# One query tile of a weights load goes as sixteen rows of 16 KB to partitions 0 to 15

## The chip, the cores and the metric

The kernel runs on one core of a Trainium2 chip. The metric is the device time of one execution in microseconds. A core has engines that run side by side: TensorE (PE, with its weight loads shown as PEld), VectorE (DVE), ScalarE (ACT), GpSimd (POOL) and SyncE (SP), which issues transfers. Sixteen DMA engines move the data between HBM and the on-chip memory of 128 partitions.

## What is computed

Two layers, each an attention over a cached sequence and a token-mixing MLP, with a residual around each, for a batch of 2 with one new token (`D = 512`):

```python
q = (x @ wq).reshape(B, Sq, Hq, Dh).transpose(0, 2, 1, 3)      # B 2, Sq 1, Hq 32, Dh 128
k, v = repeat(k_cache, 4, axis=1), repeat(v_cache, 4, axis=1)  # caches: 2 x 8 x 32768 x 128
p = softmax(einsum("bhqd,bhkd->bhqk", q, k) * Dh ** -0.5)
o = einsum("bhqk,bhkd->bhqd", p, v).transpose(0, 2, 1, 3).reshape(B, Sq, Hq * Dh) @ wo
...
x = x + A(layernorm(x), k_cache, v_cache, wq, wo)
x = x + mixer(layernorm(x), w1, b1, w2, b2)
x = x + A(layernorm(x), k_cache, v_cache, wq, wo)
x = x + mixer(layernorm(x), w1, b1, w2, b2)
```

All is float32. The two caches are 268 MB each, and both layers read them.

## The kernel before

The work is cut into 32 units, one for each layer, batch row and key head. A unit has eight chunks of keys and eight of values, 2 MB each. The four query heads of a key head are the rows of one product, so a unit needs the four queries of its head and, at its end, its head's part of the output matrix.

One large tile `mem` in the on-chip memory holds everything that is loaded. It is divided into cells of 4096 columns (16 KB in a partition): cells 0 to 8 are the ring for keys and values, cells 9 to 12 (`WCELL0`, `WCELLS`) hold weights, and 2560 columns more (`REST`) lie behind them. Most loads are four chunks at once: 128 rows of 64 KB, 8 MB. They go in one queue, SyncE's, in the order keys of a unit (4 chunks), values of the unit before (4 chunks), and so on. A load that overwrites a buffer waits on SyncE until PE has worked through what lay there; while it waits, what stands behind it on SyncE waits too.

`load_weights(k, cell)` loads the weights of two heads (`TWO_HEADS[k]`) as one transfer of 128 rows of 32 KB, 4 MB: for each head four query tiles (128 rows of `wq` by 512 columns, `DT` of them) and four output tiles (`R`). `wq_at(h)` and `wo_at(h)` find them again through `home`. The pairs 0 to 2 are loaded once in each layer, the pair 3 stays: seven loads.

The queries of a unit are made by `make_q` in four steps. Steps 0 and 1 are `q_products` with two tiles each: a matmul with the normalised input (`xnT`, 128 rows by one or two batch rows) against a query tile, 512 columns wide, summed over the four tiles into one bank. Steps 2 and 3 copy the row and turn it into columns (`L362`, `L366`, `L374`). Both batch rows of a head are made at once.

The order is written down by a small planner at build time: time is counted in chunks, `kbeg[n]` is the time of unit n's first chunk of keys, `at(time, f, ...)` notes a call, and the last loop goes through the chunks, issues each load, works off each chunk (`k_chunk` with the scores, `L426`; `v_chunk`, `L581`) and calls what is noted for that time. So steps 0 and 1 of the query for unit n stand at `kbeg[n] - 6` and `kbeg[n] - 5`, behind the second and third chunk of four chunks of keys, and a weights load stands at `kbeg[n] - 10`. On each engine the instructions run in that order.

`spot()` hands out rows of 512 columns for passing results, eight in turn in cell 8. `misc()` hands out parts of one bank.

Of the kernel before, what the change touches and what calls it, by code (L numbers as in the profile page):

```python
# [13 lines left out]
P = 128  # L14
CK = 4096
# [5 lines left out]
RING = 3  # L21
# [7 lines left out]
REST = 5  # L29
IN_PSUM = (4, 5, 3)  # L30
KEPT_Q = 4
RESIDENT = (5, 7)
TWO_HEADS = ((0, 1), (2, 3), (4, 6), RESIDENT)
FOLLOWS = {2: (2.2, -0.9, -0.8, -0.7, 3.5, -0.6, -0.5, -0.4), 5: (3.05, 0.1, 0.2, 0.3, 5.1, 3.1, 3.2, 3.3)}
PIECES = (32, 16, 8, 4, 4)
THIN = 16
# [8 lines left out]
def gqa_mixer_kernel(ctx: ExitStack, tc: tile.TileContext, x, kt, v, wqo, cols, out):  # L45
# [17 lines left out]
    nc = tc.nc  # L63
    B, D = out.shape
# [4 lines left out]
    R = wqo.shape[2] // (4 * D)  # L69
    DT = D // P  # L70
# [19 lines left out]
    sm, w0 = {}, 0  # L90
# [7 lines left out]
    W = wqo.shape[2] // 4  # L98
    assert CK == 2 * W
    WCELL0, WCELLS = RING * RING, 4  # L100
    heads = list(range(HKV))
    passing = [h for h in heads if h not in RESIDENT]
    home = {}
    mem = const.tile([P, (WCELL0 + WCELLS) * CK + REST * QT * DH], F32, name="mem")

    def cells(k, m=1):
        return mem[:, k * CK : (k + m) * CK]

    def wq_at(h):
        return cells(home[h])[:, :W].rearrange("p (t c) -> p t c", t=DT)  # L110

    def wo_at(h):
        return cells(home[h])[:, W:].rearrange("p (t c) -> p t c", t=R)

    def load_weights(k, cell):
        for j in range(2):
            home[TWO_HEADS[k][j]] = cell + j
        nc.sync.dma_start(cells(cell, 2), wqo[k])


    busy = [0] * 2 * (WCELL0 + WCELLS + 1)
    now = [0]
# [72 lines left out]
    ident = sm["ident"]  # L195
# [84 lines left out]
    N1 = len(units) - 1  # L280
# [5 lines left out]
    N3 = len(units) - 1  # L286
# [7 lines left out]
    xnT = sm["xn"].rearrange("p (d b) -> p d b", b=B)  # L294
# [5 lines left out]
    spots = [0]  # L300

    def spot():

        spots[0] += 1
        return cells(RING * RING - 1)[:, spots[0] % (CK // D) * D :][:, :D]

    def to_columns(key):

# [12 lines left out]
    def unit_of(n):  # L321

        return units[n]

    q_ps, q_row, q_kept = {}, {}, {}
    kept_q = [0]

    def partner(n):

        layer, b, h = unit_of(n)  # L330
        return units.index((layer, B - 1, h)) if b == 0 and (layer == 0 or h in passing) else None

    def q_products(n, *ds):

        layer, b, h = unit_of(n)
        m = 1 if partner(n) is None else B
        for d in ds:
            if d == 0:
                q_ps[n] = bcast if N1 < n <= N3 + 2 else kept[0]
            nc.tensor.matmul(  # L340
                q_ps[n][:m, :],
                xnT[:, d, b : b + m],
                wq_at(h)[:, d, :],
                start=(d == 0),
                stop=(d == DT - 1),
            )

    def make_q(n, step, place=None):

# [8 lines left out]
        if step < 2:  # L358
            q_products(n, 2 * step, 2 * step + 1)
# [329 lines left out]
    ln = sm["ln"]  # L689
# [238 lines left out]
    kbeg, k_done, vbeg, v_done, vend_of, v_from, v_to, brings, starts, t = {}, {}, {}, {}, {}, {}, {}, [], [], 0  # L928
# [13 lines left out]
    def at(time, f, *a, rank=1):  # L942
        done.setdefault(time, []).append((rank, f, a))

    HC = NCH // HALVES
    opens = {two[0]: k for k, two in enumerate(TWO_HEADS)}
    mixed = {}
    for n in range(NU):
        layer, b, h = unit_of(n)
# [19 lines left out]
                assert max(v_done[n - 2, c] for c in range(HC)) <= q2  # L969
        if n and h in opens and (units[n] == (0, 0, h) or h in passing and units[n] == (1, 0, h)):  # L970
            at(kbeg[n] - (7 if n == N3 + 2 else 10), load_weights, opens[h], WCELL0 + opens[h] % 2 * 2)
        if n in (N1 + 1, N2 + 1):
            at(kend - 0.5, turn_scores, n, 0, rank=2)
            at(kend, q_products, n + 1, 0)
            at(kend, max_1, n)
            at(kend, q_products, n + 1, 1)
            at(kend, max_2, n)
            at(kend, exponentials_at_once, n, 0)
            at(kend, q_products, n + 1, 2, 3)
            t1 = kend + 2  # L980
            assert mixed[units[n - 1][:2]] == kend == kbeg[n + 1] - 2
            at(t1, turn_scores, n, 1, rank=2)
            at(t1, exponentials_at_once, n, 1, rank=2)
            at(t1 + 1, sums, n)
            assert t1 + 1 < v_done[n, HC] - 1
        else:
            t1 = max(kend + 2, ahead + (2 if urgent else 4))
            e = kend if N1 < n <= N3 else kend + 2
            at(max(kend, e - 1), max_1, n)
            at(e, max_2, n)  # L990
            t0 = max(k_done[n, HC - 1], *(v_done[n - 1, c] for c in range(HC) if n), 0)
            if n in (N2, N3):
                t0 = max(t0, kbeg[n + 1] - 3)
            at(t0, turn_scores, n, 0)
            at(e, exponentials, n, 0)
            if n == NU - 1:
                t1 = ahead
                assert t1 >= kend + 2 and vbeg[n] == ahead
            at(t1, turn_scores, n, 1)
            at(t1, exponentials, n, 1)  # L1000
# [74 lines left out]
    t = 0  # L1075
# [11 lines left out]
    assert not done, sorted(done)  # L1087


def _layout(A_x, A_k_cache, A_v_cache, A_wq, A_wo, B_w1, B_b1, B_w2, B_b2):  # L1090

    import numpy as np

    B, HKV, SK, DH = A_k_cache.shape
    D = A_x.shape[-1]
    n = SK // CK


    keys = np.arange(SK).reshape(n, CK)
    for c0, m in GROUPS:  # L1100
        keys[c0 : c0 + m] = keys[c0 : c0 + m].reshape(P, m, CK // P).transpose(1, 0, 2).reshape(m, CK)
    k = keys.reshape(n // PACK, PACK // 2, 2, NG, 32, JT // QT, QT // SUB, SUB)
# [11 lines left out]
    return {  # L1114
        "x": np.ascontiguousarray(A_x.reshape(B * (D // P), P).T),
        "kt": kt,
        "v": A_v_cache.reshape(B * HKV, SK * DH),
        "wqo": np.stack([np.concatenate([wqo[h] for h in two], axis=1) for two in TWO_HEADS]),
        "cols": np.concatenate(cols, axis=1),
    }  # L1120

# [24 lines left out]
```

## Time and profile before

| | |
|---|---|
| runs | 2490.39, 2491.54, 2491.6 us; median 2491.54 |
| the profiled execution | 2490.09 us, its span 2488.0 us |
| mean granted TensorE clock | 0.772 |
| busy PE, PEld, DVE, ACT | 1371.4, 376.2, 244.9, 187.7 us |
| moved | 1062.51 MB, 427 GB/s on the mean |
| `L426` (scores) | x4096, 631.7 us busy |
| `L581` (values) | x4088, 596.8 us busy |
| `L340` (query products) | x104 into `kept`, x40 into `bcast` |

The page gives the busy time of each engine, then the span in forty slices, the DMA queues, the chain of work that ended last, and groups of instructions by line. A float32 matmul stands as two records, so 2048 matmuls of scores are 4096 rows. The timeline merges equal instructions that follow each other; a number in brackets is the idle time of the engine ahead of them. The idle time of an engine that isn't the bottleneck costs nothing.

### The profile page before, as it was taken

Reading aid. Unit: us, or ns where it says so; the run is one execution under the profiler, and the core shown is the slowest. Engines: PE = TensorE matmul, PEld = TensorE weight load, DVE = VectorE, ACT = ScalarE, POOL = GpSimd, SP = SyncE. Lnnn points to the kernel's source line nnn. Section 1 sums busy time; section 2 is a strip of 40 time slices with the busy share of each in tenths; the row PEclk is TensorE's granted clock in tenths of the full one; section 3 lists DMA queues with packets and bytes.
Section 4 is the critical chain, followed back from the end, with each engine's and each line's share of the span. In section 5 each row is a group of like instructions: output and inputs, shape, how many; then the busy total and the mean of one; then the engine's idle time right before and its main releaser. Section 6 shows DMA issues by size and latency. Waiting matters only on the chain.

```text
span 2488.0 us, 20543 instructions
## 1 busy us (share of the span) xinstructions
PE 1371.4 (55%) x9302; PEld 376.2 (15%) x9302; DVE 244.9 (10%) x643; ACT 187.7 (8%) x554; POOL 4.9 (0%) x17
## 2 busy tenths in 40 slices
PE   4544445544545454657677665455455465455546
PEld 1111111111111111111121121111111111111112
DVE  1000000000000000003113110000000000010002
ACT  0000000000000000002012000000000000011002
POOL 0000000000000000000000000000000000000000
PEclk8777767876777777778888887777678677777878
DMA  9999999999999999999999999999999999999996
GB/s 421 437 432 428 433 436 430 434 435 427 436 436 432 426 436 431 427 431 407 433 427 417 428 432 432 438 430 431 432 428 438 428 429 435 431 434 431 432 431 291
DMA packets 30336, 1062.51 MB, mean 427 GB/s; under 512 B 3621, under 2 KB 3625, under 8 KB 4266
## 3 DMA queue, kind: packets, MB, share of 16 engines
q1 hardware_dynamic: 29960, 1061.17, 99.1%
q8 instruction: 73, 1.20, 0.2%
q14 instruction: 13, 0.11, 0.0%
q10 hardware_dynamic: 290, 0.04, 0.0%
HBM read 1061.19 MB, written 0.00 MB: 427 GB/s over the span
## 4 chain that ended last, share of the span: by engine, by line
DMA 73%; PE 25%; DVE 1%; issue 0%; another core or an unknown queue 0%; ACT 0%; SPq 0%; POOL 0%; ACTq 0%
DMA mem<-in_v_dram 64%; PE acc L581 20%; DMA mem<-in_kt_dram 9%; PE scores L426 3%; PE small L612 0%; PE small L455 0%; PE small L449 0%; PE bcast L340 0%; ACT S L466 0%; PE small L642 0%; PE kept L246 0%; PE kept L792 0%; PE bcast L672 0%; DVE S L551 0%
## 5 line engine op out<-in xcount | busy, mean ns | idle before, releaser
L426 PE MATMUL scores<-mem,small_sb 128*32 128x512 f32 x4096 | 631.7, 736 | 605.4 <-DMA mem<-in_kt_dram 605.2
L581 PE MATMUL acc<-mem,S 128*16 128x512 f32 x4088 | 596.8, 723 | 457.1 <-DMA mem<-in_v_dram 447.7
L426 PEld LDWEIGHTS scores<-mem,small_sb 128*32 128x32 f32 x4096 | 150.0, 129 | 988.7 <-issue 903.7
L466 ACT ACTIVATE S<-S,small_sb 128x128 f32<-128x128 f32 x240 | 123.4, 517 | 2107.9 <-DVE small_sb L457 1556.9
L581 PEld LDWEIGHTS acc<-mem,S 128*16 128x16 f32 x4088 | 132.6, 109 | 810.8 <-issue 664.4
L441 DVE TENSOR_REDUCE small_sb<-scores 128x1 f32<-128x512 f32 x64 | 44.2, 691 | 819.5 <-PE scores L426 819.5
L461 DVE STREAM_TRANSPOSE S<-scores 128x512 f32<-128x512 f32 x64 | 45.5, 710 | 116.0 <-PE acc L581 116.0
L340 PE MATMUL kept<-mem,small_sb 128*2 128x512 f32 x104 | 51.1, 617 | 1.7 <-DVE small_sb L274 1.7
L466 ACT ACTIVATION_READ_ACCUMULATOR S<-S,small_sb 128x1 f32 x240 | 44.7, 186 | 0.0
L246 PE MATMUL kept<-mem,small_sb 128*1 128x512 f32 (+1 forms) x236 | 42.4, 598 | 2.6 <-ACT mem L835 2.4
L451 DVE TENSOR_REDUCE small_sb<-small 1x4 f32<-1x128 f32 x32 | 8.9, 279 | 277.7 <-PE small L449 277.7
L614 DVE RECIPROCAL small_sb<-small 128x4 f32<-128x4 f32 x32 | 5.9, 185 | 304.6 <-PE small L612 304.6
L623 DVE TENSOR_TENSOR small_sb<-small,small_sb 128x4 f32<-128x4 f32 x31 | 5.1, 164 | 295.8 <-PE small L621 295.8
L551 DVE SCALAR_TENSOR_TENSOR S<-acc,small_sb,S 128x128 f32<-128x128 f32 x93 | 32.6, 351 | 3.3
L835 ACT ACTIVATE S<-bcast,small_sb 128x512 f32<-128x512 f32 x28 | 21.5, 777 | 87.2 <-DVE small_sb L704 85.1
L366 PE MATMUL small<-small_sb,mem 2*128 2x2 f32 x112 | 15.5, 256 | 17.9 <-DVE mem L362 17.9
L549 DVE TENSOR_SCALAR S<-acc,small_sb 128x128 f32<-128x128 f32 x31 | 10.8, 350 | 147.3 <-PE acc L581 147.3
L621 PEld LDWEIGHTS small<-small_sb,S 128*128 128x128 f32 x62 | 12.7, 258 | 48.8 <-issue 41.2
L340 PE MATMUL bcast<-mem,small_sb 128*1 128x512 f32 (+1 forms) x40 | 19.4, 600 | 0.0
L366 PEld LDWEIGHTS small<-small_sb,mem 2*128 2x128 f32 x112 | 14.3, 196 | 30.5 <-DVE mem L362 27.3
L852 DVE SCALAR_TENSOR_TENSOR acc<-S,small_sb,acc 128x512 f32<-128x512 f32 x24 | 18.1, 755 | 2.5
L449 PE MATMUL small<-small_sb 128*1 128x128 f32 x64 | 16.6, 353 | 3.1 <-DVE small_sb L447 3.1
(147 smaller groups left out, 285.3 us busy)
## 6 DMA issues: line engine op xcount, KB each, us to landing
mem<-in_kt_dram SPq DMA_DIRECT2D x14, 4096.0 KB, 22.5
mem<-in_v_dram SPq DMA_DIRECT2D x11, 4096.0 KB, 29.2
mem<-in_wqo_dram SPq DMA_DIRECT2D x7, 4096.0 KB, 37.6
mem<-in_v_dram SPq DMA_DIRECT2D x13, 2048.0 KB, 21.3
mem<-in_kt_dram SPq DMA_DIRECT2D x12, 2048.0 KB, 19.3
mem<-in_kt_dram SPq DMA_DIRECT2D x24, 1024.0 KB, 8.8
mem<-in_v_dram SPq DMA_DIRECT2D x21, 1024.0 KB, 8.8
mem<-in_kt_dram SPq DMA_DIRECT2D x2, 6144.0 KB, 24.2
```

Of the source, the lines that this page charges most:

```text
L246: nc.tensor.matmul((rows if to is None else to)[32 * g : 32 * g + b + 1, :], weights if b else weights[:, 1:], row, start=to is not None, ...
L340: nc.tensor.matmul(q_ps[n][:m, :], xnT[:, d, b : b + m], wq_at(h)[:, d, :], start=(d == 0), stop=(d == DT - 1),)
L366: nc.tensor.matmul(pt[:, r * m : (r + 1) * m], q_row[n][:m, r * DH : (r + 1) * DH], ident[:m, :m], start=True, stop=True,)
L426: nc.tensor.matmul(sc_ps[n, half][32 * g : 32 * g + 32, :], q, kc[k * NG + g], start=(i == 0 and k == 0), stop=(i == PACK - 1 and k == SUB ...
L441: nc.vector.tensor_reduce(mx[n][:, half : half + 1], sc_ps[n, half], axis=AX.X, op=ALU.max)
L449: nc.tensor.matmul(pm[:1, :P], mxa, ident, start=True, stop=True)
L461: nc.vector.transpose(S[half], sc_ps[n, half])
L466: nc.scalar.activation(s[:, :, h], s[:, :, h], AF.Exp, bias=neg[n][:, h : h + 1], scale=SCALE, accum_out=lsum[n][:, half, h : h + 1],)
L551: nc.vector.scalar_tensor_tensor(t, acc[:, k * DH : (k + 1) * DH], mask[:, k : k + 1], t, op0=ALU.mult, op1=ALU.add)
L581: nc.tensor.matmul(acc[32 * g : 32 * g + R * QT, :], S[half][:, col : col + R * QT], vc[q], start=(c == v_from[n] and q < NG), stop=(c == ...
L835: nc.scalar.activation(hid[key, f], px[key], AF.Gelu_apprx_tanh, bias=shift[key][:, f : f + 1], scale=slope[key][:, f : f + 1],)
L852: nc.vector.scalar_tensor_tensor(h if f == FT - 1 else acc, h, w, acc, op0=ALU.mult, op1=ALU.add)
```

## The change

For the pairs 1 and 2 (`PART`: heads 2 and 3, heads 4 and 6), in both layers, one of the sixteen tiles leaves the weights load: the fourth query tile of the pair's first head. The load is then 128 rows of 30 KB. The tile, 128 rows of 512 columns, is laid out in HBM as sixteen rows of 4096 columns: row u holds the tile's rows u, u + 16, u + 32, ... one behind the other. `lower_tile` brings them to partitions 0 to 15 of cell 8, in four loads of four rows (partitions step, step + 4, step + 8, step + 12), one at a time at `kbeg[n] - 28`, `- 24`, `- 20` and `- 16`.

So that the product can be made, the input's last 128 rows go to partitions 0 to 15 as well: `lower_input` makes eight products with sixteen columns of the identity each and copies the result to `low`, a part of the mixer's small columns. The product for this tile is then a sum of eight, each over 16 rows. `spot()` hands out cell 8 only from unit N1 (13) to unit N3 + 4 (22), where cell 8 isn't used for the tile, and five rows of the columns behind the weights otherwise.

```diff
+PART = (1, 2)
+Q = 16
...
+    lowered = {}
+    low = sm["ln"][:Q, 16 : 16 + P // Q * B]
...
     def load_weights(k, cell):
+        tiles = 2 * (DT + R) - (k in PART)
         for j in range(2):
-            home[TWO_HEADS[k][j]] = cell + j
-        nc.sync.dma_start(cells(cell, 2), wqo[k])
+            home[TWO_HEADS[k][j]] = cell * CK + j * (DT + R - (k in PART)) * D
+        of = wqo[k].rearrange("p c -> (p c)")[: P * tiles * D].rearrange("(p c) -> p c", p=P)
+        nc.sync.dma_start(mem[:, cell * CK :][:, : tiles * D], of)
+
+    def lower_tile(k, step):
+        to = mem[:Q, (WCELL0 - 1) * CK :][:, : P // Q * D]
+        lowered[TWO_HEADS[k][0]] = to
+        of = wqo[k].rearrange("p c -> (p c)")[-P * D :].rearrange("(u c) -> u c", u=Q)
+        nc.sync.dma_start(to[step::4], of[step::4])
+
+    def lower_input():
+        p = misc()
+        for a in range(P // Q):
+            nc.tensor.matmul(
+                p[:Q, a * B : (a + 1) * B], ident[:, a * Q : (a + 1) * Q], sm["xn"][:, -B:], start=True, stop=True
+            )
+        nc.vector.tensor_copy(low, p[:Q, : P // Q * B])
...
     def spot():
         spots[0] += 1
-        return cells(RING * RING - 1)[:, spots[0] % (CK // D) * D :][:, :D]
+        inside = kbeg[N1] <= now[0] < kbeg[N3 + 4]
+        w, m = ((WCELL0 - 1) * CK, CK // D) if inside else ((WCELL0 + WCELLS) * CK, REST)
+        return mem[:, w + spots[0] % m * D :][:, :D]
...
-            nc.tensor.matmul(
-                q_ps[n][:m, :],
-                xnT[:, d, b : b + m],
-                wq_at(h)[:, d, :],
-                start=(d == 0),
-                stop=(d == DT - 1),
-            )
+            pairs = [(xnT[:, d, b : b + m], wq_at(h, d))] if h not in lowered or d < DT - 1 else [
+                (low[:, a * B + b : a * B + b + m], lowered[h][:, a * D : (a + 1) * D]) for a in range(P // Q)
+            ]
+            for i, (x, t) in enumerate(pairs):
+                nc.tensor.matmul(
+                    q_ps[n][:m, :], x, t, start=(d == 0), stop=(d == DT - 1 and i == len(pairs) - 1)
+                )
...
             at(kbeg[n] - (7 if n == N3 + 2 else 10), load_weights, opens[h], WCELL0 + opens[h] % 2 * 2)
+            if opens[h] in PART:
+                at(kbeg[n] - 28, lower_input)
+                for step in range(4):
+                    at(kbeg[n] - 28 + 4 * step, lower_tile, opens[h], step)
```

On PE, ahead of the unit that opens with head 2 in the first layer, the query products stood between the scores of the second, third and fourth chunk like this (`kept` is the bank of the queries, `acc` that of the values):

```order
L426 MATMUL scores<-mem,small_sb 32x512 x16
L340 MATMUL kept_85<-mem,small_sb 2x512 x2
L426 MATMUL scores<-mem,small_sb 32x512 x8
L340 MATMUL kept_85<-mem,small_sb 2x512 x2
L426 MATMUL scores<-mem,small_sb 32x512 x8
L366 MATMUL small<-small_sb,mem 128x2 x4
L581 MATMUL acc<-mem,S_91 16x512 x8
```

With the change (its lines are numbered otherwise: `L453` are the scores, `L371` the query products, `L393` the turn into columns, `L608` the values) the same place on PE reads:

```order
L453 MATMUL scores<-mem,small_sb 32x512 x16
L371 MATMUL kept_85<-mem,small_sb 2x512 x2
L453 MATMUL scores<-mem,small_sb 32x512 x8
L371 MATMUL kept_85<-mem,small_sb 2x512 x9
L453 MATMUL scores<-mem,small_sb 32x512 x8
L393 MATMUL small<-small_sb,mem 128x2 x4
L608 MATMUL acc<-mem,S_91 16x512 x8
```

The second group has nine matmuls where it had two; it stands ahead of the scores of the last chunk. The same is so at the other three places.

On SyncE's queue, the loads ahead of the same unit were these (`in_kt_dram` keys, `in_v_dram` values, `in_wqo_dram` weights):

```order
L139 DMA mem<-in_kt_dram 128x16384
L139 DMA mem<-in_v_dram 128x16384
L139 DMA mem<-in_kt_dram 128x16384
L139 DMA mem<-in_v_dram 128x16384
L139 DMA mem<-in_kt_dram 128x16384
L139 DMA mem<-in_v_dram 128x16384
L118 DMA mem<-in_wqo_dram 128x8192
L139 DMA mem<-in_kt_dram 128x16384
```

With the change (`L164` keys and values, `L126` weights, `L134` the four loads of rows):

```order
L164 DMA mem<-in_kt_dram 128x16384
L134 DMA mem<-in_wqo_dram 4x4096
L164 DMA mem<-in_v_dram 128x16384
L134 DMA mem<-in_wqo_dram 4x4096
L164 DMA mem<-in_kt_dram 128x16384
L134 DMA mem<-in_wqo_dram 4x4096
L164 DMA mem<-in_v_dram 128x16384
L134 DMA mem<-in_wqo_dram 4x4096
L164 DMA mem<-in_kt_dram 128x16384
L164 DMA mem<-in_v_dram 128x16384
L126 DMA mem<-in_wqo_dram 128x7680
L164 DMA mem<-in_kt_dram 128x16384
```

Each small load stands behind a load of 8 MB and ahead of the next one; the weights load has 7680 columns for 8192. Besides these, PE gets eight small products and DVE one copy four times; the order of all else is as it was.

More of the change, by code (lines that the diff above doesn't have):

```diff
@@ L107, in cells, with wq_at @@
         return mem[:, k * CK : (k + m) * CK]
-    def wq_at(h):
-        return cells(home[h])[:, :W].rearrange("p (t c) -> p t c", t=DT)
+    lowered = {}
+    low = sm["ln"][:Q, 16 : 16 + P // Q * B]
+    def wq_at(h, d):
+        return mem[:, home[h] + d * D :][:, :D]
     def wo_at(h):
-        return cells(home[h])[:, W:].rearrange("p (t c) -> p t c", t=R)
+        w = home[h] + (DT - (h in lowered)) * D
+        return mem[:, w : w + W].rearrange("p (t c) -> p t c", t=R)
     def load_weights(k, cell):
+        tiles = 2 * (DT + R) - (k in PART)
         for j in range(2):
-            home[TWO_HEADS[k][j]] = cell + j
-        nc.sync.dma_start(cells(cell, 2), wqo[k])
+            home[TWO_HEADS[k][j]] = cell * CK + j * (DT + R - (k in PART)) * D
[13 more added lines that the diff above has]
+        nc.vector.tensor_copy(low, p[:Q, : P // Q * B])
     busy = [0] * 2 * (WCELL0 + WCELLS + 1)
@@ L1087, in gqa_mixer_kernel, with _two_heads @@
     assert not done, sorted(done)
+def _two_heads(two, parted, d):
+    import numpy as np
+    if not parted:
+        return np.concatenate(two, axis=1)
+    c = np.arange((d // P - 1) * d, d // P * d)
+    main = np.concatenate([np.delete(two[0], c, axis=1), two[1]], axis=1)
+    last = two[0][:, c].reshape(P // Q, Q, d).transpose(1, 0, 2)
+    return np.concatenate([main.ravel(), last.ravel()]).reshape(P, -1)
 def _layout(A_x, A_k_cache, A_v_cache, A_wq, A_wo, B_w1, B_b1, B_w2, B_b2):
@@ L1117, in _layout @@
         "v": A_v_cache.reshape(B * HKV, SK * DH),
-        "wqo": np.stack([np.concatenate([wqo[h] for h in two], axis=1) for two in TWO_HEADS]),
+        "wqo": np.stack([_two_heads([wqo[h] for h in two], k in PART, D) for k, two in enumerate(TWO_HEADS)]),
         "cols": np.concatenate(cols, axis=1),
```

## The prediction

> **What bounds the kernel now.** I read the page first: its DMA rows, then the chain of waits.
>
> ```profile
> span 2488.0 us, 20543 instructions
> DMA  9999999999999999999999999999999999999996
> q1 hardware_dynamic: 29960, 1061.17, 99.1%
> q8 instruction: 73, 1.20, 0.2%
> DMA 73%; PE 25%; DVE 1%; issue 0%; another core or an unknown queue 0%; ACT 0%; SPq 0%; POOL 0%; ACTq 0%
> mem<-in_wqo_dram SPq DMA_DIRECT2D x7, 4096.0 KB, 37.6
> ```
>
> The transfers of SyncE's queue fill 99.1% of all sixteen engines' time, in every slice but the last. The kernel is a stream; it gets shorter only if the engine that finishes last has less to move, and longer if that stream runs dry. The 25% of PE in the chain is the work that frees a buffer before the next load can be issued; it costs nothing while an earlier load is still moving.
>
> The last microseconds of the stream, in a table of stretches (length, busy time of PE, PEld, DVE, ACT and POOL with instructions in brackets, PE clock, DMA share, GB/s), show that the sixteen engines don't finish together.
>
> ```profile
> 2466.00:2467.00 1.00, 0.57 (x8) 0.25 (x12) 0.00 (x0) 0.00 (x0) 0.00 (x0) 1.00 0.92 367
> 2467.00:2468.00 1.00, 1.00 (x16) 0.12 (x4) 0.00 (x0) 0.00 (x0) 0.00 (x0) 1.00 0.59 240
> 2469.00:2470.00 1.00, 0.95 (x8) 0.03 (x6) 0.00 (x0) 0.00 (x0) 0.00 (x0) 1.00 0.48 188
> 2470.00:2471.00 1.00, 0.80 (x24) 0.43 (x24) 0.91 (x3) 0.00 (x0) 0.00 (x0) 1.00 0.33 123
> ```
>
> The share falls from 0.92 to 0.48, half the engines, about 3 to 4 us before the rest stop. So some engines have spare time, which rows given to them could use.
>
> The change touches four places, the query products of the pairs that begin with heads 2 and 4, in both layers. I read the first in the timeline (start, length, engine, line, operation, and in brackets the idle time before it and what ended it), then the chain there.
>
> ```profile
> 218.77 0.43 SPq L118 DMA_DIRECT2D mem<-in_wqo_dram  x1
> 276.02 6.31 PE L426 MATMUL scores<-mem,small_sb 128*32 128x512 f32 x32 [19.72 <-DMA mem<-in_kt_dram]
> 285.57 1.45 PE L340 MATMUL kept<-mem,small_sb 128*2 128x512 f32 x3
> 286.86 0.59 PE L340 MATMUL kept<-mem,small_sb 128*2 128x512 f32 x1
> 289.25 0.33 SPq L139 DMA_DIRECT2D mem<-in_kt_dram  x1
> 295.37 3.44 PE L581 MATMUL acc<-mem,S 128*16 128x512 f32 x16 [3.73 <-DMA mem<-in_v_dram]
> ...
> 295.23 0.14 issue
> ```
>
> The 4 MB of weights have just held up the keys' load, and PE idles 19.72 us for it. At 276.02 the keys have landed and only one transfer, the values' 8 MB, is still queued; it lands at 295.23 (the last row is the chain's: landing, then 0.14 us to the matmul). Its 19.35 us are all the cover that PE has to work through four chunks of keys and the query products. SyncE can issue the next load only when that is done, at 289.25. This leaves 5.98 us. The same stands at the other three places:
>
> ```profile
> 610.11 0.33 SPq L139 DMA_DIRECT2D mem<-in_kt_dram  x1
> 616.23 3.44 PE L581 MATMUL acc<-mem,S 128*16 128x512 f32 x16 [3.73 <-DMA mem<-in_v_dram]
> ...
> 1794.39 0.33 SPq L139 DMA_DIRECT2D mem<-in_kt_dram  x1
> 1800.38 3.58 PE L581 MATMUL acc<-mem,S 128*16 128x512 f32 x16 [3.60 <-DMA mem<-in_v_dram]
> ...
> 1958.79 0.33 SPq L139 DMA_DIRECT2D mem<-in_kt_dram  x1
> 1965.32 3.62 PE L581 MATMUL acc<-mem,S 128*16 128x512 f32 x16 [3.92 <-DMA mem<-in_v_dram]
> ```
>
> With 0.14 us off the matmul's start, the landings are 616.09, 1800.24 and 1965.18, and the time left is 5.98, 5.85 and 6.39 us.
>
> **The change part by part.** *The weights load* loses 128 of its rows of 2 KB, 256 KB in all. The values' 8192 KB move in 19.35 us (276.02 to 295.37), so 256 KB are 0.60 us. Four times that is a gain of 2.4 us on every engine, and the most that the change can bring, since no other byte goes away.
>
> *The sixteen rows of 16 KB.* The 8 MB load has 128 rows of 64 KB, eight to an engine, 2.42 us each; a 16 KB row takes 0.60 us. What matters is which engines move them. The one transfer of the trace with four rows is the output's, and this is its window:
>
> ```profile
> DMA packets 8, 0.00 MB, mean 1 GB/s; under 512 B 4, under 2 KB 8, under 8 KB 8
> ```
>
> Eight packets: four of 512 B and four smaller ones, which I read as one count of the semaphore for each engine. Four rows went to four engines, then, and not to sixteen. If the four loads use the same four engines, these get 4 x 0.60 = 2.4 us more and 0.6 less, +1.8 us at each place, while the other twelve get -0.6. [...] If the four were among those with spare time, the landing at each place moves by -0.6; if they were among the last, by +1.8. But a lead is lost when the stream runs dry, which the next paragraph expects at each place, and then they have little to give at the next. I take the middle, +0.6 a place, +2.4 in all, with -2.4 and +7.2 as the ends.
>
> *The query products.* In step 1 of the first head of each pair, two matmuls of 512 columns become nine: seven more. A float32 matmul stands in the trace as two records, and the four records of the two old products start 0.43 us apart (285.57, three of them, and 286.86). Seven more are 14 x 0.43 = 6.0 us. They contract over 16 rows where those did over 128, and no row shows that shape; the columns that stream through are as many, so I take the same price. Above it lies 14 x 0.59 = 8.3 us, were they not to overlap; below it, little, were they to run side by side. The clock at the place is full:
>
> ```profile
> 276.00:282.00 6.00, 5.98 (x32) 1.65 (x33) 0.00 (x0) 0.00 (x0) 0.00 (x0) 0.55 1.00 429
> 286.00:288.00 2.00, 2.00 (x18) 0.61 (x17) 0.00 (x0) 0.00 (x0) 0.00 (x0) 1.00 0.83 360
> ```
>
> PE is busy without a gap in both, so nothing hides them; the idle 19.72 us lie ahead of the keys and can't be used, since the order is fixed. The scores of the last chunk are queued behind them on PE, SyncE's load waits for these scores, and the sixteen engines wait for SyncE. The issue moves from 289.25 to 295.3, when the values have just landed: the 5.98 us are gone.
>
> An issue isn't a transfer. What a start from an empty queue costs, the beginning of the run shows:
>
> ```profile
> 0.74 0.39 SPq L118 DMA_DIRECT2D mem<-in_wqo_dram  x1
> 1.00:1.70 0.70, 0.00 (x0) 0.00 (x0) 0.32 (x2) 0.04 (x1) 0.53 (x5) 1.00 0.00 0
> 1.70:2.00 0.30, 0.00 (x0) 0.00 (x0) 0.27 (x3) 0.30 (x1) 0.00 (x0) 1.00 4.47 1201
> 1.19 31.32 DMA mem<-in_kt_dram
> ```
>
> Issued at 0.74, the first packets start after 1.70: 1.0 us at least. The weights and the keys behind them, 12 MB, take 29.0 us at the rate above, and the keys land at 32.51 (1.19 + 31.32), where 29.8 would be due: 2.7 us from an issue to what a stream without a break would have brought. I take 2.7, since it is from landing to landing as the places are, with 1.0 as the lower end. So each place is late by issue + 6.0 + 2.7 less the old landing: 2.7, 2.7, 2.85 and 2.3 us, 10.6 in all; with 1.0 it is 3.8.
>
> *The input turned to sixteen rows.* Eight products of 16x2 and one copy stand four times behind the last scores of a keys' load, which has by then released its buffer. The place before the first:
>
> ```profile
> 169.52 4.94 PE L581 MATMUL acc<-mem,S 128*16 128x512 f32 x32 [8.63 <-DMA mem<-in_v_dram]
> 174.39 0.39 PE L612 MATMUL small<-small_sb 128*128 128x4 f32 x2
> ```
>
> One small product takes up to 0.39 us, so eight take at most 3.1, and PE idles 8.63 us there: nothing. Without that cover they would cost 3 us each time.
>
> *SyncE's queue* gets sixteen more issues of about 0.4 us (0.39 above), each right behind a load and ahead of one that waits microseconds for PE; the buffer they write was last read long before. Nothing. The scratch rows that move to other columns keep their instructions.
>
> The sum: +10.6 for four dry starts, +2.4 for where the rows go (the lighter load is in it) = +13.0. The profiled execution took 2490.09 us, of which the span is 2488.0 and 2.1 lie around it; 2490.1 + 13.0 = 2503.1. The median of the runs shown is 2491.54, 1.45 above, which the range covers.
>
> **The rivals.** *The products are covered* (the other side). If the seven extra matmuls take no more than 5.98 - 2.7 = 3.3 us of PE's time, the next load is in the queue in time, no start is dry, and what is left is the lighter load on engines with a lead of 3 to 4 us: 2490.1 - 2.4 = 2487.7. For it speaks the tail, where half the engines wait. It decides at 0.23 us a record, and the trace has 0.43 for the same columns. [...]
>
> *The four engines are the late ones.* Instruction fetches (73 packets in the page) go through the same engines, and half end late. If some of the four are among these, the full +1.8 counts at each place: 10.6 + 7.2 = 17.8, 2507.9. The tail speaks for it, since half the engines are late; that no row names them leaves it open.
>
> *The rows don't gather* (the change doesn't do what it says): four rows are dealt to other engines each time. Then bytes and balance are as before, and the dry starts alone remain: 2500.7. The output's eight packets fit this too.
>
> **How the numbers follow.** A measurement of this kernel can tell about 0.2%, 5 us, from no change. Forecast (dry starts, four engines, 2503) 0.58; late engines 0.14; rows don't gather 0.10; covered 0.18. The forecast's own range is from 3.8 - 2.4 = +1.4 (2491.5) to 10.6 + 7.2 = +17.8 (2508); it leaves some 0.07 under 5 us. The covered case lies within 0.2%; that its gain is larger than 2.4 I give 0.03. So faster 0.03, same 0.22, slower 0.75. The range from 2489.5 to 2510 leaves out the covered case and an unforeseen rest.
>
> **What would show it.** Right: in the changed kernel's timeline the nine products' eighteen records at 0.43 us, SyncE's keys' load about 6 us later behind the keys' first scores (19 us instead of 13.2), and the keys' landing 22 us, not 19.35, after the values'; the DMA share dips there four times. Wrong: products in less than half that time, or a keys' load that still lands 19.35 us after the values; a shorter stream with a tail of less than 3 us would be the covered case, and a landing late already ahead of the products the late engines.

## The result, and the profile after

The changed kernel takes 2517.57 us (median of 4 runs, 2516.28 to 2518.41), the kernel before 2491.08 in the same comparison (four runs of each): a ratio of 1.0106, 95% interval [1.0089, 1.0124]. It is slower, as forecast, but by 26.5 us instead of 13.0, and outside the range. The profiled execution took 2517.83 us.

The page of the changed kernel: its span, the DMA share in 40 slices, the share of SyncE's queue, and the chain of waits.

```profile
span 2516.0 us, 20809 instructions
DMA  9999999999999999999999999999899999999996
q1 hardware_dynamic: 30088, 1061.17, 98.1%
DMA 71%; PE 28%; DVE 0%; issue 0%; ACT 0%; SPq 0%; ACTq 0%
```

The queue's share fell from 99.1% to 98.1%: the stream now has holes. 98.1% of 2516.0 and 99.1% of 2488.0 are nearly the same time of moving (2468 and 2466 us). So nothing moves noticeably slower, and the time went into waiting.

The first of the four places, in the timeline and at its end in the chain:

```profile
277.17 6.44 PE L453 MATMUL scores<-mem,small_sb 128*32 128x512 f32 x32 [19.28 <-DMA mem<-in_kt_dram]
286.85 9.56 PE L371 MATMUL kept<-mem,small_sb 128*2 128x512 f32 x18
296.35 3.64 PE L453 MATMUL scores<-mem,small_sb 128*32 128x512 f32 x16
300.05 0.33 SPq L164 DMA_DIRECT2D mem<-in_kt_dram  x1
323.26 3.64 PE L453 MATMUL scores<-mem,small_sb 128*32 128x512 f32 x16 [11.52 <-DMA mem<-in_kt_dram]
...
300.05 23.08 DMA mem<-in_kt_dram
```

The eighteen records of step 1 take 9.56 us, 0.53 each on average. Behind them the last chunk's scores take 3.64 us. SyncE issues the next keys' load 22.88 us after the keys' first scores (300.05 less 277.17), where it was 13.23, and from issue to landing it takes 23.08 us. From the first scores of one keys' load to those of the next there are 46.09 us at this place. The other three:

```profile
604.90 6.42 PE L453 MATMUL scores<-mem,small_sb 128*32 128x512 f32 x32 [19.32 <-DMA mem<-in_kt_dram]
627.78 0.33 SPq L164 DMA_DIRECT2D mem<-in_kt_dram  x1
650.95 3.64 PE L453 MATMUL scores<-mem,small_sb 128*32 128x512 f32 x16 [11.41 <-DMA mem<-in_kt_dram]
...
1795.46 5.06 PE L453 MATMUL scores<-mem,small_sb 128*32 128x512 f32 x32 [18.96 <-DMA mem<-in_kt_dram]
1818.34 0.33 SPq L164 DMA_DIRECT2D mem<-in_kt_dram  x1
1840.36 3.64 PE L453 MATMUL scores<-mem,small_sb 128*32 128x512 f32 x16 [12.01 <-DMA mem<-in_kt_dram]
...
1967.86 5.90 PE L453 MATMUL scores<-mem,small_sb 128*32 128x512 f32 x32 [18.13 <-DMA mem<-in_kt_dram]
1990.74 0.33 SPq L164 DMA_DIRECT2D mem<-in_kt_dram  x1
2013.89 3.35 PE L453 MATMUL scores<-mem,small_sb 128*32 128x512 f32 x16 [9.43 <-DMA mem<-in_kt_dram]
```

In the kernel before, the first scores of the same loads (the first place's began at 276.02) and of the next ones were these:

```profile
314.72 3.64 PE L426 MATMUL scores<-mem,small_sb 128*32 128x512 f32 x16 [10.13 <-DMA mem<-in_kt_dram]
...
596.89 6.30 PE L426 MATMUL scores<-mem,small_sb 128*32 128x512 f32 x32 [19.73 <-DMA mem<-in_kt_dram]
635.59 1.93 PE L426 MATMUL scores<-mem,small_sb 128*32 128x512 f32 x8 [10.14 <-DMA mem<-in_kt_dram]
...
1781.03 6.44 PE L426 MATMUL scores<-mem,small_sb 128*32 128x512 f32 x32 [19.59 <-DMA mem<-in_kt_dram]
1819.74 2.79 PE L426 MATMUL scores<-mem,small_sb 128*32 128x512 f32 x12 [10.00 <-DMA mem<-in_kt_dram]
...
1945.97 5.89 PE L426 MATMUL scores<-mem,small_sb 128*32 128x512 f32 x32 [20.29 <-DMA mem<-in_kt_dram]
1985.62 3.64 PE L426 MATMUL scores<-mem,small_sb 128*32 128x512 f32 x16 [9.80 <-DMA mem<-in_kt_dram]
```

The issue now stands 22.88 us behind the first scores at all four. The stretches of 46.09, 46.05, 44.90 and 46.03 us were 38.70, 38.70, 38.71 and 39.65, so the four places lose 7.39, 7.35, 6.19 and 6.38: 27.3 of the 28.0 us by which the span grew.

Why the products took so long stands in the stretches of the first place (length, busy time of PE, PEld, DVE, ACT and POOL, granted clock of TensorE, DMA share, GB/s), and in the weight loads of single records (start, length, and in brackets the pause before):

```profile
288.00:290.00 2.00, 2.00 (x6) 0.37 (x5) 0.00 (x0) 0.00 (x0) 0.00 (x0) 1.00 0.98 426
292.00:294.00 2.00, 2.00 (x5) 0.36 (x4) 0.00 (x0) 0.00 (x0) 0.00 (x0) 0.78 0.31 131
294.00:296.00 2.00, 2.00 (x3) 0.12 (x1) 0.00 (x0) 0.00 (x0) 0.00 (x0) 0.50 0.00 0
298.00:300.00 2.00, 1.99 (x12) 0.20 (x4) 0.00 (x0) 0.00 (x0) 0.00 (x0) 0.52 0.00 0
...
292.53 0.08 PEld L371 LDWEIGHTS kept<-mem,small_sb 16*2 16x2 f32 x1 [0.35 <-issue]
292.95 0.08 PEld L371 LDWEIGHTS kept<-mem,small_sb 16*2 16x2 f32 x1 [0.35 <-issue]
293.66 0.12 PEld L371 LDWEIGHTS kept<-mem,small_sb 16*2 16x2 f32 x1 [0.62 <-issue]
294.51 0.12 PEld L371 LDWEIGHTS kept<-mem,small_sb 16*2 16x2 f32 x1 [0.73 <-issue]
```

TensorE is busy without a gap, and yet its clock falls in the middle of the burst, from 1.00 to 0.78 and 0.50. The records are 0.43 us apart up to 292.95 (292.53 to 292.95, for one), as forecast, and 0.85 behind it (293.66 to 294.51). The last records and the last chunk's scores run at a clock of 0.50 to 0.52. The DMA share is 0.00 from 294 us to the issue at 300.05: the stream is dry.

### The profile page after: what moved, and what is told of

It is laid out like the page before. It is cut to its first block, busy times and chain, and to the rows that moved or that the text cites. A ratio compares the mean times of both kernels' runs of the same rounds, so it can differ in the third digit from the quotient of the medians.

```text
span 2516.0 us, 20809 instructions
## 1 busy us (share of the span) xinstructions
PE 1417.8 (56%) x9422; PEld 383.4 (15%) x9422; DVE 245.3 (10%) x647; ACT 188.1 (7%) x554; POOL 4.9 (0%) x17
## 3 DMA queue, kind: packets, MB, share of 16 engines
q1 hardware_dynamic: 30088, 1061.17, 98.1%
## 4 chain that ended last, share of the span: by engine, by line
DMA 71%; PE 28%; DVE 0%; issue 0%; ACT 0%; SPq 0%; ACTq 0%
DMA mem<-in_kt_dram 36%; DMA mem<-in_v_dram 35%; PE acc L608 12%; PE scores L453 12%; PE kept L371 2%; PE kept L271 1%; ACT S L493 0%; PE small L648 0%; PE small L482 0%; PE small L639 0%; PE small L669 0%; PE small L393 0%; PE bcast L371 0%; PE kept L819 0%; PE small L476 0%
## 5 line engine op out<-in xcount | busy, mean ns | idle before, releaser
L453 PE MATMUL scores<-mem,small_sb 128*32 128x512 f32 x4096 | 636.5, 744 | 606.3 <-DMA mem<-in_kt_dram 606.1
L608 PE MATMUL acc<-mem,S 128*16 128x512 f32 x4088 | 600.5, 727 | 438.0 <-DMA mem<-in_v_dram 428.6
L453 PEld LDWEIGHTS scores<-mem,small_sb 128*32 128x32 f32 x4096 | 149.7, 129 | 999.0 <-issue 911.1
L608 PEld LDWEIGHTS acc<-mem,S 128*16 128x16 f32 x4088 | 132.9, 110 | 790.7 <-issue 644.5
L371 PE MATMUL kept<-mem,small_sb 128*2 128x512 f32 (+1 forms) x160 | 82.8, 656 | 1.7 <-DVE small_sb L299 1.7
L393 PE MATMUL small<-small_sb,mem 2*128 2x2 f32 x112 | 15.5, 256 | 17.8 <-DVE mem L389 17.8
L371 PEld LDWEIGHTS kept<-mem,small_sb 128*2 128x2 f32 (+1 forms) x160 | 13.5, 87 | 62.6 <-issue 60.8
L371 PE MATMUL bcast<-mem,small_sb 128*1 128x512 f32 (+1 forms) x40 | 20.3, 623 | 0.0
L393 PEld LDWEIGHTS small<-small_sb,mem 2*128 2x128 f32 x112 | 14.3, 196 | 33.7 <-DVE mem L389 29.7
```

Source lines behind the costliest of these rows:

```text
L371: nc.tensor.matmul(q_ps[n][:m, :], x, t, start=(d == 0), stop=(d == DT - 1 and i == len(pairs) - 1))
L393: nc.tensor.matmul(pt[:, r * m : (r + 1) * m], q_row[n][:m, r * DH : (r + 1) * DH], ident[:m, :m], start=True, stop=True,)
L453: nc.tensor.matmul(sc_ps[n, half][32 * g : 32 * g + 32, :], q, kc[k * NG + g], start=(i == 0 and k == 0), stop=(i == PACK - 1 and k == SUB ...
L608: nc.tensor.matmul(acc[32 * g : 32 * g + R * QT, :], S[half][:, col : col + R * QT], vc[q], start=(c == v_from[n] and q < NG), stop=(c == ...
```

## The experiments

Theory A, formed from these rows: the whole loss comes from the extra products, by a late issue, and half of it because the clock falls while they run. Rivals: the rows of 16 KB hold the stream up (B), or a 16-row product is dear in itself (C).

**One product (e1).** In q_products:

```
-  ... for a in range(P // Q)
+  ... for a in range(1)
```

> The changed kernel with only one of the eight 16-row products of each parted tile (seven eighths of that tile are left out of the queries); every load, the turned input and the order stay. Theory A (the whole loss comes from TensorE's extra products at the four places: they push SyncE's keys' load behind the end of the values, and the clock falls to half while they run): the load is issued 13.2 us after the keys' first scores again, the keys land 19.3 to 19.5 us after the values, and the time is that of the kernel before less 0 to 2.4 us for the lighter loads: 2488 to 2491. Theory B (the rows of 16 KB, dealt to the same four engines, hold the stream up at each place): most of the loss stays, over 2505. Theory C (a 16-row product is dear in itself): as A here, told apart by the next runs.

2489.50 us, ratio to the kernel before 0.9989 [0.9980, 0.9999]. With every load and the turned input in place the loss is gone, and a little more. B falls. The issue at the first place:

```profile
277.23 5.04 PE L453 MATMUL scores<-mem,small_sb 128*32 128x512 f32 x32 [18.99 <-DMA mem<-in_kt_dram]
289.39 0.33 SPq L164 DMA_DIRECT2D mem<-in_kt_dram  x1
315.94 3.64 PE L453 MATMUL scores<-mem,small_sb 128*32 128x512 f32 x16 [9.72 <-DMA mem<-in_kt_dram]
```

The issue comes 12.16 us after the first scores (12.1 to 13.7 over the four places), and the next ones 38.71 us after them, as before the change. C falls by the trace of the changed kernel: its 16-row records are 0.43 us apart for as long as the clock is full, as those of 128 rows.

**Eight products of 128 rows (e2), and seven with 32 columns (e3).**

```
-  (low[:, a * B + b : ...], lowered[h][:, a * D : (a + 1) * D]) for a in range(P // Q)
+  (xnT[:, d - 1, b : b + m], wq_at(h, d - 1)) for a in range(P // Q)      # e2
+  ... for a in range(1), and ahead of it, seven times,                    # e3
+  matmul(kept[1][:32, :], ident[:, :32], wq_at(h, d - 1), start=True, stop=True)
```

> The changed kernel with the eight 16-row products replaced by eight products of 128 rows with the tile before (that tile counts eight times and the parted tile not at all); as many matmuls of 512 columns, two columns of weights each, same loads. Theory A: the records are as long as the 16-row ones, 0.43 us at full clock and 0.85 at half, the issue stands about 22.9 us behind the keys' first scores, and the time is the changed kernel's, 2515 to 2520, if the clock falls for the narrow weights (two columns) or simply for the length of the burst; if it falls because only 16 rows of the array work, the clock stays full here, the issue moves to 19.2 us and the time to some 2503. Theory C: 14 records at 0.43, 2503. Theory B: 2517, as after.

> The changed kernel with one of the eight 16-row products kept and the other seven replaced by products of 128 rows with 32 columns of weights (columns of the identity, into a bank that nobody reads), the shape of the scores; as many matmuls of 512 columns (seven eighths of the parted tile are left out of the queries). If the clock falls because the products use two columns of the array, it stays full here: issue 19.2 us behind the keys' first scores, 4 x 3.65 us less than the changed kernel, about 2503. If it falls a fixed time (10 us) after it rose, whatever runs, the issue stays at 22.9 us and the time at 2517. Theory B: 2517.

2502.67 us, ratio 1.0040 [1.0025, 1.0055], and 2500.62, ratio 1.0036 [1.0022, 1.0050]. They are 15 and 17 us under the changed kernel, with as many records. The timeline of e2 at the first place, and two of its stretches:

```profile
277.28 5.37 PE L453 MATMUL scores<-mem,small_sb 128*32 128x512 f32 x32 [18.66 <-DMA mem<-in_kt_dram]
285.89 7.46 PE L371 MATMUL kept<-mem,small_sb 128*2 128x512 f32 x17
295.58 0.33 SPq L164 DMA_DIRECT2D mem<-in_kt_dram  x1
...
292.00:294.00 2.00, 2.00 (x15) 0.50 (x16) 0.00 (x0) 0.00 (x0) 0.00 (x0) 1.00 0.38 164
294.00:296.00 2.00, 1.50 (x10) 0.22 (x2) 0.41 (x1) 0.00 (x0) 0.00 (x0) 1.00 0.00 0
```

The clock stays at 1.00, seventeen records take 7.46 us (0.43 apart), and the issue comes 18.30 us after the first scores. That is 6.14 behind e1's 12.16, beside the prediction's 14 x 0.43 = 6.0; at the other three places it is 5.1, 5.1 and 6.0 behind, since the clock doesn't rise at the same time after the first scores in both runs (2.7 to 5.9 us in e1, 3.0 to 4.5 in e2). So two columns of weights didn't make the clock fall here, nor did seventeen records in a row: e2 has both, at 1.00. What is left of the differences to the changed kernel is the number of rows, and the place from which they are read.

**Of 32 and of 64 rows (e6, e7).** As e2, with `xnT[:32, ...]` and `wq_at(h, d - 1)[:32]`, or 64.

> The run with eight products of the tile before, but of its first 32 rows instead of 128 (the queries are not the reference's). If the clock falls with the number of rows of the array at work, and 32 are as few as 16: clock 0.50 from some 6 us after the products began, issue 22.9 us behind the keys' first scores, 2517. If only the separate place or partitions of the 16 rows do it, or 32 rows are enough: clock full throughout, issue at 18.3 us, 2503.

> The same with 64 rows. If the clock follows the share of the array's rows at work, somewhere between 16 and 128 it stays full: I expect it here, issue at 18.3 us, 2503; if not, 22.9 us and 2517.

2516.97 us, ratio 1.0104 [1.0084, 1.0124], and 2501.50, ratio 1.0045 [1.0029, 1.0061]. The stretch from 292 to 294 us of e6, then of e7:

```profile
292.00:294.00 2.00, 2.00 (x4) 0.25 (x2) 0.00 (x0) 0.00 (x0) 0.00 (x0) 0.50 0.30 131
...
292.00:294.00 2.00, 2.00 (x6) 0.33 (x4) 0.00 (x0) 0.00 (x0) 0.00 (x0) 1.00 0.31 131
```

TensorE is fully busy in both, and both read the tile that e2 reads, so the place is not the cause. With 32 rows the clock is at 0.50, as with 16 in the changed kernel (294 to 296 us); with 64 it is at 1.00, as with 128. The clock's own records in the traces say the same of all four places: it was full for 10.24 us at each of them in the changed kernel and in e6, and fell 7 to 10 us ahead of the issue; in e2 and e7 it stayed full for 17.07 us, past the issue.

The loss from the clock is 14.9 us by the medians of the changed kernel and e2. By the issues it is more: they stand 22.88 us behind the first scores four times, in e2 18.30, 18.78, 18.24 and 18.05, 18.2 us less in sum. The profiled execution of e2 lost some 4 us elsewhere in the stream; why, no row here shows.

**Five products (e5).** `range(5)`.

> The changed kernel with five of the eight 16-row products (three eighths of the parted tile are left out of the queries): four matmuls, eight records, more than before. At 0.43 us a record the load is issued 3.4 us later than before, 2.5 us ahead of the values' landing. By the prediction's cover (5.98 us less 2.7 for a start) this costs 0.1 us a place: the time of the one-product run, 2489.5. By the 3.7 us from issue to what an unbroken stream would bring, which the places of the changed kernel show, it costs 1.2 us a place, 4.6 in all: some 2494, and the keys land 20.5 us after the values instead of 19.35. If the clock falls already after five products, 0.43 us for each record behind the fall come on top.

2496.95 us, ratio 1.0024 [1.0015, 1.0033], above both sums. The first place, from the products to the landing:

```profile
286.11 5.40 PE L371 MATMUL kept<-mem,small_sb 128*2 128x512 f32 x12
291.44 3.60 PE L453 MATMUL scores<-mem,small_sb 128*32 128x512 f32 x16
295.08 0.33 SPq L164 DMA_DIRECT2D mem<-in_kt_dram  x1
...
295.08 22.90 DMA mem<-in_kt_dram
```

The products are done at full clock, but it falls just behind them (0.89 on the mean from 290 to 292 us, 0.50 from 292 to 294) and the scores take 3.60 us. This is the case that the expectation's last sentence names. The issue comes 17.86 us after the first scores (277.22) instead of the 15.6 that eight records behind e1's 12.16 would give. From issue to landing it is 22.90 us, 3.5 more than the 19.36 of a load that is already queued; e2 shows 23.06, the changed kernel 23.08. An issue should therefore come some 3.6 us ahead of the landing before it, or the stream is late; this is worked out from these durations, and no run places an issue just there. The prediction's 2.7 was too little.

**The products ahead of the keys (e4, e9), and that order without the change (e10).** The eleven matmuls of both steps go ahead of the keys' first scores, where TensorE idles 19 us and the weights have landed:

```
+  if h in opens and opens[h] in PART and layer_opens(n):    # the first head of the two pairs, in its first unit of a layer
+      q0 = q1 = kbeg[n] - 8                                 # was kbeg[n] - 6 and kbeg[n] - 5
```

> The changed kernel, all of it computed, with the query products of the four heads' pairs (eleven matmuls) ahead of the first scores of the same keys' load, in the time in which TensorE waits for these keys; the weights land some 9 us before the keys. Theory A: nothing of the products is left behind the keys' first scores, the load is issued about 11.5 us after them, no start is dry, and the time is that of the kernel before less 0 to 2.4 us: 2488 to 2491. If the weights land too late for that, the products push the scores by a few us and the cover of 6 us takes it: the same time. Theory B: over 2505.

> The early-products version once more with more runs: by theory A it keeps the gain of the lighter loads alone, 0.5 to 2.4 us under the kernel before (ratio 0.9990 to 0.9998); if the lead was chance, 1.0000.

> The kernel before with nothing changed but the query products of the same four places moved ahead of the keys' first scores. The keys' load is issued some 3 us earlier, but an earlier load is still moving then, so nothing should be gained: 2490.5 to 2492, ratio 1.0000. If the move itself is what gains in the early version, it shows here: 2489.5.

e4 took 2489.88 us, ratio 0.9990 [0.9981, 1.0000]; e9, the same kernel with more runs, 2489.52, ratio 0.9994 [0.9985, 1.0003]; e10 2491.49, ratio 1.0002 [0.9993, 1.0011]. Here is e4's first place:

```profile
259.05 13.37 PE L371 MATMUL kept<-mem,small_sb 128*2 128x512 f32 x22
277.36 9.34 PE L453 MATMUL scores<-mem,small_sb 128*32 128x512 f32 x64 [4.93 <-DMA mem<-in_kt_dram]
286.75 0.33 SPq L164 DMA_DIRECT2D mem<-in_kt_dram  x1
```

All of the changed kernel's work is done here. The 22 records take 13.37 us, 0.61 each where 0.43 is the distance at full clock, end 4.9 us ahead of the keys, and nothing of it reaches the path. The order alone gains nothing (e10). What is left is the lighter load, by elimination: 1 to 2 us in these two, but e4's interval ends at 1.0000 and e9's holds it. The tail of e1, which has the same loads, and then that of e4:

```profile
2467.00:2468.00 1.00, 0.52 (x8) 0.00 (x0) 0.00 (x0) 0.00 (x0) 0.00 (x0) 1.00 0.72 287
2468.00:2469.00 1.00, 0.90 (x8) 0.13 (x8) 0.00 (x0) 0.00 (x0) 0.00 (x0) 1.00 0.69 264
...
2467.00:2468.00 1.00, 0.42 (x8) 0.13 (x8) 0.00 (x0) 0.00 (x0) 0.00 (x0) 1.00 0.63 248
2468.00:2469.00 1.00, 0.82 (x12) 0.10 (x8) 0.22 (x1) 0.00 (x0) 0.00 (x0) 1.00 0.44 164
```

Before, the share stood at 0.48 in the last us but one of the stream. In e1 it stands at 0.69, as if the engines that had waited at the end now carried some of the rest; e4's 0.44 doesn't show that. Where the 1 to 2 us come from stays open.

**How the rows are loaded (e8, e11 to e16).** All of them keep the products off the path: e8, e11, e13, e15 and e16 are the early version, e12 and e14 keep one product of the tile before.

```
   to[step::4], of[step::4]                                   # e4: four loads, partitions 0, 4, 8, 12, rows 64 KB apart
-> to, of                                                     # e8: one load of 16 rows
-> to[step::2], of[step::2]                                   # e11: two loads of 8
-> mem[::8, ...], of                                          # e12: one load, to partitions 0, 8, ... 120
-> mem[::8, ...], 16 rows of keys 64 KB apart                 # e14
-> to[4 * step : 4 * step + 4], of[4 * step : 4 * step + 4]   # e13: neighbours in both
-> to[step::4], of[4 * step : 4 * step + 4]                   # e15: neighbours in memory alone
-> to[4 * step : 4 * step + 4], of[step::4]                   # e16: neighbouring partitions alone
```

> The early-products version with the sixteen rows in one load instead of four loads of four. If four rows go to the same four engines each time and these had time to spare, that was worth up to 2.4 us (0.6 us at each of the four places for the twelve others): here every engine gets one row of 16 KB, what it moves is as much as before the change, and the time is that of the kernel before, 2490 to 2492. If the rows of the four loads did not gather, the time stays that of the early version, 2488 to 2490.

> The early-products version with the sixteen rows in two loads of eight. The one load of sixteen rows cost 12 us over four loads of four, and its packets of 16 KB took 4 us each instead of 0.6. If that is because sixteen engines write into the same sixteen partitions at once (256 KB at some 60 GB/s), eight at once are held up half as much, twice as often: 2494 to 2502. If only a load of exactly sixteen rows is bad, 2489 to 2491.

> One load of sixteen rows, but to the partitions 0, 8, 16 and so on to 120; the rows are not used, and one product of the tile before stands in place of the eight (the parted tile is left out of the queries), so that no start is dry. If the sixteen-row load is slow because its rows lie in neighbouring partitions, its packets take 0.6 us here and the time is 2490 to 2492. If a load with one row for each engine is slow wherever it goes, its packets take 4 us again and the time is 2500 to 2504.

> The early-products version with four loads of four rows that lie next to each other in memory (16 KB apart) and go to neighbouring partitions, instead of every fourth row (64 KB apart). If the distance decides, four neighbours delay each other: some us over the early version's 2489.5, up to 2502. If the number of rows in a load decides, as the early version: 2488 to 2491.

> One load of sixteen rows of 16 KB to partitions 0, 8, 16 and so on, as in the run before, but read from the start of sixteen rows of keys, 64 KB apart, instead of from one piece of 256 KB (rows not used; one product of the tile before in place of the eight). If the distance decides, the stall is gone: 2490 to 2492. If sixteen engines with one row each are slow by themselves, 2499 to 2502 again.

> The early-products version with four loads of four rows that lie next to each other in memory, but go to partitions four apart (the sixteen rows arrive in another order, so the queries are not the reference's). If nearness in memory is what costs: as the run with neighbours in both, 2510 to 2513. If nearness of the partitions is: 2488 to 2491. In between if both count.

> The other half: rows 64 KB apart in memory to four neighbouring partitions (again in another order). If nearness in memory is what costs: 2488 to 2491. If nearness of the partitions is: 2510 to 2513.

| run | rows a load, partitions | us | ratio to before |
|---|---|---|---|
| e4 | 4, four apart | 2489.88 | 0.9990 [0.9981, 1.0000] |
| e15 | 4, four apart (rows near in memory) | 2489.45 | 0.9989 [0.9980, 0.9998] |
| e13 | 4, neighbours | 2511.76 | 1.0086 [1.0070, 1.0103] |
| e16 | 4, neighbours (rows far in memory) | 2511.71 | 1.0074 [1.0057, 1.0091] |
| e11 | 8, two apart | 2501.82 | 1.0045 [1.0032, 1.0059] |
| e8 | 16, neighbours | 2502.16 | 1.0049 [1.0032, 1.0066] |
| e12 | 16, eight apart | 2499.74 | 1.0035 [1.0022, 1.0049] |
| e14 | 16, eight apart (rows far in memory) | 2499.34 | 1.0035 [1.0022, 1.0048] |

e8 missed both of its forecasts and e13 came 10 us above its highest. My first reading of e8 and e11, that rows near in memory collide, fell with e14 and e15: memory distance changes 0.4 us at most (e15 2489.45 for e4's 2489.88, e14 2499.34 for e12's 2499.74, e16 2511.71 for e13's 2511.76). For loads of four rows the partitions decide: e13 and e16 lose 22 us to e4 and e15, 1.4 us for each of their sixteen loads. The stretch in which the first of these loads moves, in e15 and then in e16:

```profile
146.00:152.00 6.00, 1.92 (x12) 0.68 (x16) 0.00 (x0) 0.00 (x0) 0.00 (x0) 0.55 0.91 393
...
146.00:152.00 6.00, 0.21 (x4) 0.23 (x8) 0.00 (x0) 0.00 (x0) 0.00 (x0) 0.54 0.95 306
```

The engines are as busy (0.91 and 0.95) and move a fifth less. The packet records of the traces show which packets are slow, and that the expectations of e11 and e12 read e8 wrongly: its 16 KB rows took 0.7 to 1.9 us, not 4. The time goes into the 64 KB rows of the big loads beside them. These take 2.42 us as a rule; over 3 us took 12 to 19 of them in the kernel before, e4 and e15, but 183 and 195 in e16 and e13, and 105 to 120 in e8, e11, e12 and e14, with up to 5.0 us for one row.

What eight or sixteen rows cost isn't explained by the spacing alone: e12's rows lie eight apart and cost 2.5 us a load, where four rows four apart cost nothing that shows (e4, e15); e12 takes 2.4 us less in all than e8, whose sixteen rows go to neighbours. How the number of rows in a load and their partitions make up these prices, and why neighbours are dear, no run shows.

## Why the prediction was wrong

**The dry starts** came at all four places, as it said, and nowhere else. Its mechanism held; two of its prices did not.

**The price of the products** is the step that failed. It took 14 x 0.43 us because the clock at the place was full. That row, 286 to 288 us, was the clock of other instructions. The new ones run longer, and in them, with 16 rows, the clock fell to 0.50 (294 to 296 us). At the first place the last four or so of the eighteen records were 0.85 us apart, and the last chunk's scores behind them ran at 0.50 to 0.52 too. The prediction had the issue 19 us behind the first scores; it came at 22.88, which is 3.65, 3.66, 3.52 and 4.06 us late at the four places. With 128 rows (e2) it comes at 18.30 at the first place, with seventeen records in 7.46 us: the price was right for the shape from whose row it was taken. That e2's time, 2502.67, lies next to the 2503.1 forecast is partly luck, since there the start was priced too low and the sixteen rows too high. The prediction saw that no row shows 16 rows, but its higher price, 14 x 0.59, kept the clock full as well, and not even that one went into the range, which ended at 2510.

**The start from an empty queue** was taken from the run's beginning, 2.7 us. It is 3.7 at three of the places and 2.5 at the third (21.88 us from issue to landing less 19.36), for which no run shows the reason. The four places lost 27.3 us where 10.6 were forecast, 16.7 more: 14.9 are the late issues (the four numbers above), the remaining 1.8 the start.

**The sixteen rows** were given +2.4 us, between -2.4 and +7.2. The runs without dry starts (e1, e4, e9, e15) are 1.3 to 2.8 us under the kernel before, so there the truth lay near the lower end, about 4 us under the middle. In the changed kernel itself all but the four places is 0.7 us longer by the spans and 0.8 shorter by the medians, so whether it keeps that gain isn't shown. Nor is the prediction's reason for it, engines with spare time at the end: the tails of e1 and e4 differ. What it didn't consider is that where the rows land could cost more than the +2.4 that it gave to which engine carries them: from e4 to e16, the same rows in memory on other partitions, it is 22 us.

The sum by the measured sizes: 10.6 + 16.7 = 27.3 for the four places, and nothing that can be told from the noise for the rest, against 26.5 between the medians and 28.0 between the spans.

**The turned input and the sixteen issues** cost nothing that shows, as it said: e4 and e9 contain both and take 2489.88 and 2489.52 us.

**The rivals.** "The products are covered" was the wrong picture of this kernel, but its price without dry starts, 2487.7, is near what e9 reaches when the products really are covered (2489.5). That rows don't gather falls: the semaphore records of the traces show four completions for each of these loads, and the time from the first to the last of the sixteen completions of a big load grows with them (e4: 1.9 us ahead of the first, 3.8 behind the fourth; in the kernel before it stays at 1.9). "The four engines are the late ones" falls as a price, since e1 with the same loads isn't above the kernel before, where this rival adds 7.2 us. But the sign that the prediction names for it came at the first place: by the longer spread the four engines were the last there, and the keys landed 1.15 us later than before, ahead of the products (first scores at 277.17 for 276.02; 277.00 to 277.36 in e1, e4, e9 and e15). By the end of the stream it was made up; how, no run shows.

## What to carry to other kernels

The clock that a row showed here was that of its own instructions, 1.00 from 286 to 288 us in the kernel before and 0.50 from 294 to 296 us with the 16-row products of the changed kernel: when work is added to a burst, price it with the shape that will run and at both clocks, up to the end of everything queued behind it. Before a load is delayed, measure the cover to the moment at which its issue must stand, some 3.6 us ahead of the landing here, and not to the landing itself. Work that only needs early data belongs in the idle time ahead of the critical load, not behind it: that alone turned 26 us more into no loss, or 1 to 2 us less.

## What the runs showed of the hardware that was not expected

TensorE's clock went with the number of rows that the added products contract over, not only with whether it is busy: in these bursts of nine products and the scores around them, without a gap (2.00 us busy of 2.00 from 292 to 294 us in all four), it fell to 0.50 with 16 (the changed kernel) and 32 rows (e6) and stayed at 1.00 up to the issue with 64 (e7) and 128 (e2).

A load of four rows of 16 KB in a full stream was free or dear by the spacing of its partitions: nothing that shows at four apart (e4, e15), 1.4 us each to four neighbours (e13, e16). Against e4, eight rows two apart in one load cost 1.5 us (e11), sixteen in one load 2.5 (eight apart, e12) to 3.1 us (neighbours, e8). The price shows in the big rows that move beside them: 105 to 195 rows of 64 KB took over 3 us in the dear runs and 12 to 19 in e4, e15 and the kernel before, while the 16 KB rows of e8 took 0.7 to 1.9 us.
